# Two products of a fused attention, experts and gated-block kernel computed with seven block products in place of eight

## The chip, the cores and the metric

The kernel runs on one core of one Trainium2 chip. The metric is the device time of one execution in microseconds; times are compared as medians of several runs. One execution is also recorded by the profiler, and all rows below come from that one.

## The reference

Three stages work on 4608 tokens of 512 features. Only the third is touched by the change.

```python
attn_out = _attn_ref(q, k, v)                     # softmaxed q times (softmaxed k^T v)
x = attn_out.transpose(0, 2, 1, 3).reshape(4608, 512)
x = _moe_ref(x, modality_id, w_gate, modality_bias, w1, w2)   # one of 8 experts per token

def _moe2_ref(x, w1, w2, w3, w_out):              # 512x1024, 512x1024, 1024x1024, 1024x512
    a = x @ w1
    b = x @ w2
    h = a * b @ w3
    return (h @ w_out).astype(np.float32)
```

## The kernel before

Every float32 number that enters a large matmul is held as a high part `h` and a low part `l` (`split`, lines 833 to 835: ScalarE casts the source to the high part, then VectorE subtracts it from the source to give the low part). A product is three matmuls, high by high, low by high and high by low (`PAIRS`, line 32). A matmul takes a block of 128 by 128 as its stationary operand and streams up to 512 columns.

All steps are put into a list with estimated costs, their reads and their writes (`Plan.add`), and a list scheduler puts each engine's steps into the order in which they would start (`Plan.order`). Each engine then runs its steps in that order; waits between engines follow from the data. `P` is TensorE, `S` ScalarE, `V` VectorE, `G` GpSimd, `D` the DMAs that SyncE issues, in order, and `X` a step without an instruction.

The attention stage writes `x_dram`. The expert stage (`slot`, its matmuls on lines 645 and 665) writes its result, turned, to `yT` in DRAM (line 669). `doubles` (lines 684 to 692) turns the float64 weights of the third stage into float32 in DRAM beside it, in tiles `st`, `T`, `Q`, `O`.

The third stage first builds `w3 @ w_out`, of 1024 by 512. `stage` loads weight rows into a ring of seven tiles of 1024 columns. `turned(fb)` transposes block `fb` of `w3` on TensorE (line 849) into two PSUM banks, and `split` puts its high and low parts into one of two buffers. `product(fb)` multiplies it with `w_out` (24 matmuls on line 862), and `split` puts the result into `WP`. `first_two` loads and splits `w1` and `w2` meanwhile, a row block for each `fb`. There are eight `fb`.

Then nine units of 512 tokens follow. `positions(u)` loads one unit of `yT` and splits it. For each of eight blocks `m` of 128 features of the 1024, 12 matmuls make `a` (line 914, evicted by ScalarE on line 919) and 12 more make `b`; VectorE multiplies the two (line 921) and the product is split into `PT` (lines 834, 835). Then four blocks of 128 tokens take 24 matmuls each with `WP` (line 933), ScalarE evicts them (line 939), and GpSimd issues an indirect DMA that puts the rows at their places in the output (line 941).

## Time and profile before

| what | value |
|---|---|
| runs, median of 3 (lowest to highest) | 1299.66 us (1293.59 to 1301.91) |
| profiled execution, its own time | 1293.58 us |
| its span | 1291.9 us |
| TensorE busy | 1196.3 us, 93% |
| VectorE busy | 636.1 us, 49% |
| ScalarE busy | 450.2 us, 35% |
| GpSimd busy | 292.5 us, 23% |
| mean granted TensorE clock | 0.966 of full speed |

PE is TensorE's matmuls, PEld its loads of stationary operands, DVE VectorE, ACT ScalarE, POOL GpSimd, SP SyncE. Matmuls are pipelined: the records of two that follow each other overlap, so the rate is read from start to start or from a chain, not from the duration of one. Instructions of DVE and ACT overlap a little as well, so a run of them is shorter than the sum of its records.

### The profile page before, as it was taken

Reading aid. Unit: us, or ns where it says so; the run is one execution under the profiler, and the core shown is the slowest. Engines: PE = TensorE matmul, PEld = TensorE weight load, DVE = VectorE, ACT = ScalarE, POOL = GpSimd, SP = SyncE. Lnnn points to the kernel's source line nnn. Section 1 sums busy time; section 2 is a strip of 40 time slices with the busy share of each in tenths; the row PEclk is TensorE's granted clock in tenths of the full one; section 3 lists DMA queues with packets and bytes.
Section 4 is the critical chain, followed back from the end, with each engine's and each line's share of the span. In section 5 each row is a group of like instructions: output and inputs, shape, how many; then the busy total and the mean of one; then the engine's idle time right before and its main releaser. Section 6 shows DMA issues by size and latency. Waiting matters only on the chain.

```text
span 1291.9 us, 19827 instructions
## 1 busy us (share of the span) xinstructions
PE 1196.3 (93%) x8035; PEld 1007.5 (78%) x8035; DVE 636.1 (49%) x1100; ACT 450.2 (35%) x841; POOL 292.5 (23%) x286
## 2 busy tenths in 40 slices
...
GB/s 355 392 260 69 53 244 130 250 211 208 138 127 188 204 235 136 222 271 157 207 145 33 15 51 6 60 2 64 1 66 1 65 1 65 1 65 1 33 1 33
DMA packets 67960, 153.94 MB, mean 119 GB/s; under 512 B 11758, under 2 KB 14354, under 8 KB 67858
## 3 DMA queue, kind: packets, MB, share of 16 engines
...
HBM read 129.67 MB, written 39.70 MB: 131 GB/s over the span
## 4 chain that ended last, share of the span: by engine, by line
PE 68%; DVE 2%; issue 1%; ACT 1%; DMA 0%; POOLq 0%; ACTq 0%; DVEq 0%
PE pb L914 30%; PE pb L933 15%; PE pb L665 11%; PE pb L645 8%; PE pb L862 3%; DVE w2l L591 1%; PE pb L628 1%; PE pb L849 0%; DVE xt L688 0%; ACT w2h L589 0%; DVE xt L686 0%; DVE hTl L650 0%; DMA out_dram<-misc,oall 0%; DVE xt L687 0%; DVE xt L685 0%
## 5 line engine op out<-in xcount | busy, mean ns | idle before, releaser
L921 DVE TENSOR_TENSOR xg<-xg,pb 128x512 f32<-128x512 f32 x72 | 49.5, 688 | 405.8 <-PE pb L914 400.5
L941 POOL DMA_INDIRECT out_dram<-misc,oall x36 | 35.0, 973 | 626.4 <-ACT misc L939 626.4
L645 PE MATMUL pb<-xTh,w1h 128*128 128x512 f32 (+1 forms) x384 | 134.5, 350 | 3.9 <-DVE hTl L650 3.9
L665 PE MATMUL pb<-hTh,w2h 128*128 128x512 f32 (+1 forms) x384 | 134.6, 350 | 0.0
L665 PE MATMUL pb<-hTl,w2h 128*128 128x512 f32 (+1 forms) x384 | 133.4, 347 | 0.0
L645 PE MATMUL pb<-xTl,w1h 128*128 128x512 f32 (+1 forms) x384 | 133.3, 347 | 0.1
L665 PE MATMUL pb<-hTh,w2l 128*128 128x512 f32 (+1 forms) x384 | 133.2, 347 | 0.0
L645 PE MATMUL pb<-xTh,w1l 128*128 128x512 f32 (+1 forms) x384 | 132.9, 346 | 0.0
L834 ACT CAST pTh<-xg 128x512 fp32r<-128x512 f32 x76 | 46.9, 620 | 197.3 <-DVE xg L921 197.3
L914 PE MATMUL pb<-xTh,hTh 128*128 128x512 f32 x288 | 112.1, 389 | 0.0
L914 PE MATMUL pb<-xTl,hTh 128*128 128x512 f32 x288 | 112.0, 389 | 0.0
L914 PE MATMUL pb<-xTh,hTl 128*128 128x512 f32 x288 | 112.0, 389 | 0.0
L914 PE MATMUL pb<-xTh,w1h 128*128 128x512 f32 x288 | 112.0, 389 | 0.0
L914 PE MATMUL pb<-xTl,w1h 128*128 128x512 f32 x288 | 112.0, 389 | 0.0
L914 PE MATMUL pb<-xTh,w1l 128*128 128x512 f32 x288 | 112.0, 389 | 0.0
L933 PE MATMUL pb<-w2h,pTh 128*128 128x512 f32 x288 | 112.0, 389 | 0.0
L933 PE MATMUL pb<-w2l,pTh 128*128 128x512 f32 x288 | 112.0, 389 | 0.0
L933 PE MATMUL pb<-w2h,pTl 128*128 128x512 f32 x288 | 112.0, 389 | 0.0
L649 ACT ACTIVATE hTh<-pb 128x512 fp32r<-128x512 f32 (+1 forms) x96 | 48.9, 510 | 116.8 <-PE pb L645 116.4
L645 PEld LDWEIGHTS pb<-xTh,w1h 128*128 128x128 f32 x384 | 73.1, 190 | 14.1 <-DVE hTl L650 5.1
L645 PEld LDWEIGHTS pb<-xTl,w1h 128*128 128x128 f32 x384 | 73.1, 190 | 9.4 <-DVE xTl L633 0.6
L665 PEld LDWEIGHTS pb<-hTh,w2l 128*128 128x128 f32 x384 | 73.1, 190 | 9.1
...
## 6 DMA issues: line engine op xcount, KB each, us to landing
...
```

Of the source, the lines that this page charges most:

```text
L591: P.add(g, c, lambda: e.tensor_tensor(lo(), raw(), hi().bitcast(F32), op=ALU.subtract), r=[K(nm + "r", i), K(nm + "h", i), extra], w=[K(nm ...
L628: PE.transpose(p[:, kk, 128 * t : 128 * t + 128], xg[h][:, t, c : c + 128], ident)
L645: PE.matmul(p(), lhsT=W1(i)[:, TURN[kk], ms], rhs=XT(z)[:, kk, cols], start=(kk == 0 and c == 0), stop=(kk == 3 and c == 2))
L649: P.add("S", ps_(N), lambda hh=hh, p=p: SC.activation(hh(), p(), AF.Relu), r=[K("bk", pb), "Mb"], w=[K("hh", h, m) for h in hs])
L665: PE.matmul(p(), lhsT=W2(i)[:, f, ns], rhs=HT(y)[:, f, cols], start=(f == 0 and c == 0), stop=(f == 7 and c == 2))
L834: P.add("S", (ps_ if psum else sb_)(n), lambda: SC.copy(hi(), src), r=sk, w=[hk])
L862: PE.matmul(bank[pb], lhsT=th[i][:, 8 * p2 + g], rhs=PT(y)[:, g], start=(g == 0 and n == 0), stop=(g == 7 and n == 2))
L914: PE.matmul(dst, lhsT=mat[i][:, kk, ms], rhs=XT[z][:, kk], start=(c == 0), stop=(c == 11))
L921: P.add("V", vt_(512), lambda a_=a_, p_=p_, p2=p2: V.tensor_tensor(p_, a_, bank[p2], op=ALU.mult), r=[K("bk", p2), K("a", wb), K("ring", 1 ...
L933: PE.matmul(bank[pb], lhsT=PT(i)[:, f, ts], rhs=WP[y][:, f], start=(c == 0), stop=(c == 23))
L941: P.add("G", (1.04, 0.74), lambda o3=o3, c=c: G.indirect_dma_start(out=out, out_offset=bass.IndirectOffsetOnAxis(ap=oall[:, c : c + 1], ax ...
```

## The change

`x @ w1` and `x @ w2` are each cut into two by two blocks and computed by Strassen's algorithm in Winograd's form: seven block products in place of eight, with four sums of weight blocks, four sums of token blocks, and seven sums of products. The unit is 768 tokens, six units in all; the two halves of a unit (384 tokens each) are the column blocks, the two halves of the 512 features the inner blocks.

`factors(a, t)` takes the place of `first_two`. It is called four times, for `fb` 0 to 3, loads two ring tiles, makes four sums on GpSimd, and splits seven factors of 512 columns each (28 splits in all, where there were 16). They lie in `ar`, one tile that takes the place of the expert stage's weight and activation tiles. The ring has five tiles, now all carved from one tile `ca`, which also holds the staging tiles of the earlier stages (`xt`, `xg` and smaller ones).

`positions(b)` loads the four blocks of a unit, makes four differences on VectorE and splits seven blocks of 768 columns (2 by 384). There is one set of these split blocks.

`quarter(b, f, a)` computes 128 features of both halves of the 1024 for both token halves: seven products of six matmuls of 384 columns each into four banks, and their sums. `a` 0 is `x @ w1`, `a` 1 is `x @ w2`, and with `a` 1 the sums are multiplied into those of `a` 0. Two sets of four banks alternate. The result goes to `p_dram` in DRAM.

`w3 @ w_out` goes to `wp_dram` in DRAM, copied by ScalarE. After the sixth unit a phase of its own loads `wp_dram` and, in chunks of 512 tokens by 512 features, `p_dram`, splits both (`arrive`, `weights`, `tokens`), and does the nine times four blocks of 24 matmuls as before, with four banks in place of two and two sets of split products.

Other parts of the diff only rename or place tiles: `ones` in the pool of the even batches, `w_out`'s split parts and the turned `w3` in `al`, `thm` and `tt`.

```diff
+CA, FILL, AL = 9440, 20, 9216
+BT = 768
+HB = BT // 2
...
+    wp_dram = dr.tile([1024, 512], F32, name="wp_dram")
+    p_dram = dr.tile([1024, NTOK], F32, name="p_dram")
...
+        ar = M["ar"] = pb.tile([128, 28672], F32R, name="ar")
+        part = lambda a, k, f: ar[:, a : a + k * f].rearrange("p (k f) -> p k f", k=k)
+        M["W1"] = [part(4096 * i, 4, 1024) for i in range(2)]
+        M["XT"] = [part(8192 + 2048 * i, 4, 512) for i in range(2)]
+        M["W2"] = [part(12288 + 4096 * i, 8, 512) for i in range(2)]
+        M["HT"] = [part(20480 + 4096 * i, 8, 512) for i in range(2)]
+        M["thm"] = pb.tile([128, 2 * BT], F32R, name="thm")
         M["pb"] = pb
+        M["py"] = tc.alloc_tile_pool(name="yo", bufs=1, side="right", reuse_waits="tile")
+        M["yo"] = M["py"].tile([128, 4, 2 * TS], F32, name="yo")
...
+    ar = M["ar"]
...
+    def wide_a():
         M["pr"].release()
         M["pm"] = tc.alloc_tile_pool(name="moe2", bufs=1, reuse_waits="tile")
-        M["PT"] = [M["pm"].tile([128, 8, 512], F32R, name=f"pT{i}") for i in "hl"]
-
...
+        M["al"] = M["pm"].tile([128, AL], F32R, name="al")
+
+    def wide_b():
+        M["py"].release()
+        M["pt"] = tc.alloc_tile_pool(name="turn", bufs=1, side="right", reuse_waits="tile")
+        M["tt"] = M["pt"].tile([128, 2048], F32R, name="tt")
+
+    def wide_c():
+        M["pt"].release()
+        M["px"] = tc.alloc_tile_pool(name="sums", bufs=1, side="right", reuse_waits="tile")
+        M["sx"] = M["px"].tile([128, 4 * HB], F32, name="sx")
+
+    P.add("X", 0.0, wide_a, w=two("w1r", 8) + two("w2r", 8) + ["Mc"])
+    P.add("X", 0.0, wide_b, w=[K("yo", b, i) for b in range(2) for i in range(4)] + ["Me"])
+    hand_over(["Mc"], two("wo", 8) + two("wol", 8) + [K("th", 0), K("tl", 0)])
+    hand_over(["Me"], [K(x, i) for x in ("th", "tl") for i in (2, 3)])
+    old = [K(x, i) for x in ("w1h", "w1l", "w2h", "w2l") for i in range(8)] + [K(x, b, i) for x in ("hh", "hl") for b in range(2) for i in range(8)]
+    old += [K("xh", b, i) for b in range(2) for i in range(2)] + [K("xl", b, i, "t") for b in range(2) for i in range(2)]
+    hand_over(old, two("Mf", 4))
+    hand_over([K(x, i) for x in ("st", "T", "Q", "O") for i in range(2)] + [K("xg", b, i) for b in range(2) for i in range(2)], two("ring", 5) + two("tmp", 4) + two("ev", 2))
+    ring = [(ca[:, 1024 * i : 1024 * i + 1024], [K("ring", i)]) for i in range(5)]
+    tmp = [flat(ca[:, 5120 + 512 * i : 5632 + 512 * i], 4) for i in range(4)]
+    evict = [ca[:, 8416 + 512 * i : 8928 + 512 * i] for i in range(2)]
+    WO = lambda i, g: M["al"][:, 1024 * g + 512 * i : 1024 * g + 512 * i + 512]
+
+    def th(i, q, g=0, n=4):
+        t, a = (("al", 8192), ("thm", 0), ("tt", 0), ("tt", 1024))[q]
+        a += 512 * i + 128 * g
+        return flat(M[t][:, a : a + 128 * n], n)
...
-        t, kk = ring[rot("ring", 7)]
+        t, kk = ring[rot("ring", 5)]
...
-                for g in range(4 * z, 4 * z + 4):
+                for g in range(4):
                     for n, (i, y) in enumerate(PAIRS):
-                        PE.matmul(bank[pb], lhsT=th[i][:, 8 * p2 + g], rhs=PT(y)[:, g], start=(g == 0 and n == 0), stop=(g == 7 and n == 2))
...
+                        PE.matmul(bank[pb], lhsT=th(i, 2 * p2 + z, g, 1)[:, 0], rhs=WO(y, 4 * z + g), start=(z == 0 and g == 0 and n == 0), stop=(z == 1 and g == 3 and n == 2))
+
+            P.add("P", 2.73, mm, r=[K(x, 2 * p2 + z) for x in ("th", "tl")] + [K(x, g) for g in range(4 * z, 4 * z + 4) for x in ("wo", "wol")], w=[K("bk", pb)])
+        P.add("S", ps_(512), lambda: SC.copy(evict[p2], bank[pb]), r=[K("bk", pb)], w=[K("ev", p2)])
+        P.add("D", 0.7, lambda: SP.dma_start(wp_dram[128 * fb : 128 * fb + 128], evict[p2]), r=[K("ev", p2)], w=[K("wpd", fb)])
...
+    A11, A12, A22, S1, S2, S3, S4 = range(7)
+    B11, T1, T3, T2, B21, B22, T4 = range(7)
+    PRODUCTS = ((A11, B11, 0), (S1, T1, 2), (S3, T3, 3), (S2, T2, 1), (A12, B21, 0), (S4, B22, 2), (A22, T4, 3))
+    Mt = ar[:, 0:28672].rearrange("p (f a i s t c) -> p f a i s t c", f=4, a=2, i=2, s=7, t=2)
+
+    def factors(a, t):
+
+
+        r0, k0 = stage(f"m{a + 1}", t)
+        r1, k1 = stage(f"m{a + 1}", t + 2)
+        mk = lambda i, m: K("M", a, t, i, m)
+        at = lambda i, m: Mt[:, :, a, i, m, t]
+        q = {A11: flat(r0[:, 0:512], 4), A12: flat(r1[:, 0:512], 4), A22: flat(r1[:, 512:1024], 4)}
+        a21 = flat(r0[:, 512:1024], 4)
+        both = k0 + k1
+        sk = {A11: both, A12: both, A22: both}
+
+        def sum_(n, m, x, y, op, r):
+            P.add("G", gt_(512), lambda: G.tensor_tensor(tmp[n], x, y, op=op), r=r, w=[K("tmp", n)])
+            q[m], sk[m] = tmp[n], [K("tmp", n)]
+
+        sum_(0, S1, a21, q[A22], ALU.add, both)
+        sum_(1, S3, q[A11], a21, ALU.subtract, both)
+        sum_(2, S2, tmp[0], q[A11], ALU.subtract, both + [K("tmp", 0)])
+        sum_(3, S4, q[A12], tmp[2], ALU.subtract, both + [K("tmp", 2)])
+        for m in (A11, S1, S3, S2, A12, S4, A22):
+            P.add("S", sb_(512), lambda m=m: SC.copy(at(0, m), q[m]), r=sk[m] + two("Mf", 4), w=[mk(0, m)])
+            P.add("V", vt_(512), lambda m=m: V.tensor_tensor(at(1, m), q[m], at(0, m).bitcast(F32), op=ALU.subtract), r=sk[m] + [mk(0, m)] + two("Mf", 4), w=[mk(1, m)])
...
-        first_two(1 + fb // 4, fb % 4)
...
+        if fb < 4:
+            factors(fb // 2, fb % 2)
...
+    P.add("X", 0.0, wide_c, w=two("th", 4) + two("tl", 4) + ["Md"])
+    hand_over(["Md"], [K("s", i) for i in (2, 3, 4, 5)] + [K("Xh", 6), K("Xl", 6)])
+    hand_over([K(x, g) for x in ("wo", "wol") for g in range(3)], [K(x, i) for x in ("Xh", "Xl") for i in (0, 1)])
+    hand_over([K(x, g) for x in ("wo", "wol") for g in range(3, 8)], [K(x, i) for x in ("Xh", "Xl") for i in range(2, 6)])
+    hand_over(two("tmp", 4), two("raw", 4))
+    hand_over(two("ring", 5), [K("raw", i) for i in (4, 5, 6)] + two("pa", 3) + [K("s", 1)])
+    hand_over(two("ev", 2), [K("pa", 3), K("s", 0)])
...
+    S_ = lambda i: sums[i] if i < 2 else M["sx"][:, HB * (i - 2) : HB * (i - 1)]
+
+    def X(i, x):
+        t, n = (M["thm"], i) if x == T4 else (M["al"], 2 * x + i)
+        return flat(t[:, BT * n : BT * n + BT], 2)
+
+    RAW = {B11: 0, B21: 1, B22: 2, T3: 3, T1: 4, T2: 5, T4: 6}
+    B12 = 3
+
+    def positions(b):
+        src = yT[:, BT * b : BT * b + BT].rearrange("(j n p) t -> p j n t", p=128, j=2)
+        for n, (j, k) in ((RAW[B11], (0, 0)), (B12, (0, 1)), (RAW[B22], (1, 1)), (RAW[B21], (1, 0))):
+            P.add("D", 1.2, lambda n=n, j=j, k=k: SP.dma_start(raw[n], src[:, j, :, HB * k : HB * k + HB]), r=["yT"], w=[K("raw", n)])
...
+        def diff(to, x, y):
+            P.add("V", vt_(768), lambda: V.tensor_tensor(raw[to], raw[x], raw[y], op=ALU.subtract), r=[K("raw", x), K("raw", y)], w=[K("raw", to)])
+
+        diff(RAW[T1], B12, RAW[B11])
+        diff(RAW[T3], RAW[B22], B12)
+        diff(RAW[T2], RAW[B22], RAW[T1])
+        diff(RAW[T4], RAW[B21], RAW[T2])
+        for _, x, _ in PRODUCTS:
+            n = RAW[x]
+            split(raw[n], [K("raw", n)], lambda x=x: X(0, x), lambda x=x: X(1, x), K("Xh", x), K("Xl", x), 768)
...
+    def quarter(b, f, a):
+
+
+        z = (2 * f + a) % 2
+        bk = lambda j: bank[4 * z + j][:, 0:HB]
+        bkk = lambda j: K("bk", 4 * z + j)
+        S = lambda j: S_(3 * z + j)
+        sk = lambda j: K("s", 3 * z + j)
+        seen = set()
+        for m, x, j in PRODUCTS:
+
+            def mm(m=m, x=x, j=j, fresh=j not in seen):
+                for t in range(2):
+                    for n, (i, y) in enumerate(PAIRS):
+                        PE.matmul(bk(j), lhsT=Mt[:, f, a, i, m, t], rhs=X(y, x)[:, t], start=(fresh and t == 0 and n == 0), stop=(t == 1 and n == 2), skip_group_check=not fresh)
+
+            seen.add(j)
+            P.add("P", 1.04, mm, r=[K("Mf", f), K("Xh", x), K("Xl", x)] + [K("M", a, t, i, m) for t in range(2) for i in range(2)], w=[bkk(j)])
+            for c, (mine, to) in enumerate(((A11, 0), (S1, 1), (S3, 2))):
+                if m == mine:
+                    P.add("S", ps_(HB), lambda j=j, to=to: SC.copy(S(to), bk(j)), r=[bkk(j)], w=[sk(to)])
+            if m == S2:
+                P.add("V", vt_(HB), lambda: V.tensor_tensor(S(0), S(0), bk(1), op=ALU.add), r=[bkk(1)], w=[sk(0)])
+                P.add("G", gt_(HB), lambda: G.tensor_tensor(S(1), S(1), S(2), op=ALU.add), r=[sk(2)], w=[sk(1)])
+        p0, p1 = f % 2, 2 + f % 2
+        lo, hi = slice(0, HB), slice(HB, BT)
+        o0, o1 = pa[p0], pa[p1]
+        if a == 0:
+            P.add("S", ps_(HB), lambda: SC.copy(o0[:, lo], bk(0)), r=[bkk(0)], w=[K("pa", p0)])
+            P.add("V", vt_(HB), lambda: V.tensor_tensor(o0[:, hi], S(0), bk(2), op=ALU.add), r=[sk(0), bkk(2)], w=[K("pa", p0)])
+            P.add("V", vt_(HB), lambda: V.tensor_tensor(o1[:, lo], S(0), bk(3), op=ALU.add), r=[sk(0), bkk(3)], w=[K("pa", p1)])
+            P.add("G", gt_(HB), lambda: G.tensor_tensor(o1[:, hi], S(0), S(1), op=ALU.add), r=[sk(0), sk(1)], w=[K("pa", p1)])
+        else:
+            P.add("G", gt_(HB), lambda: G.tensor_tensor(S(1), S(0), S(1), op=ALU.add), r=[sk(0)], w=[sk(1)])
+            P.add("G", gt_(HB), lambda: G.tensor_tensor(o1[:, hi], o1[:, hi], S(1), op=ALU.mult), r=[sk(1)], w=[K("pa", p1)])
+            P.add("V", vt_(HB), lambda: V.tensor_tensor(o0[:, lo], o0[:, lo], bk(0), op=ALU.mult), r=[bkk(0)], w=[K("pa", p0)])
+            P.add("V", vt_(HB), lambda: V.tensor_tensor(S(2), S(0), bk(2), op=ALU.add), r=[sk(0), bkk(2)], w=[sk(2)])
+            P.add("V", vt_(HB), lambda: V.tensor_tensor(o0[:, hi], o0[:, hi], S(2), op=ALU.mult), r=[sk(2)], w=[K("pa", p0)])
+            P.add("V", vt_(HB), lambda: V.tensor_tensor(S(2), S(0), bk(3), op=ALU.add), r=[sk(0), bkk(3)], w=[sk(2)])
+            P.add("V", vt_(HB), lambda: V.tensor_tensor(o1[:, lo], o1[:, lo], S(2), op=ALU.mult), r=[sk(2)], w=[K("pa", p1)])
+            for p_, r in ((p0, f), (p1, f + 4)):
+                P.add("D", 1.2, lambda p_=p_, r=r: SP.dma_start(p_dram[128 * r : 128 * r + 128, BT * b : BT * b + BT], pa[p_]), r=[K("pa", p_)], w=[K("pd", r, b)])
+
+    for b in range(NTOK // BT):
+        positions(b)
+        for f in range(4):
+            for a in range(2):
+                quarter(b, f, a)
...
+    hand_over(kept(0, 1), two("wph", 8))
+    hand_over(kept(1, 2), [K("ph", 0, i) for i in range(8)] + two("wpl", 8))
+    hand_over(kept(2, 3), [K("pl", 0, i) for i in range(8)] + [K("ph", 1, i) for i in range(8)])
+    hand_over(kept(3, 4), [K("pl", 1, i) for i in range(8)])
+    hand_over(two("raw", 7), two("chunk", 2) + two("o3", 2))
+    hand_over(two("pa", 4) + two("s", 2), [K("chunk", 2), K("o3", 2), K("o3", 3)])
...
+    def arrive(src, r, to, hk, lk, first):
+        n = rot("chunk", 2 if first else 3)
+        P.add("D", 2.9, lambda: SP.dma_start(chunks[n], src.rearrange("(n p) t -> p n t", p=128)), r=r, w=[K("chunk", n)])
+        for f in range(4):
+            split(chunks[n][:, f], [K("chunk", n)], lambda f=f: to(0, f), lambda f=f: to(1, f), hk(f), lk(f), 512)
+
+    def weights(h):
+        arrive(wp_dram[512 * h : 512 * h + 512], [K("wpd", 4 * h + f) for f in range(4)], lambda i, f: WP(i, 4 * h + f), lambda f: K("wph", 4 * h + f), lambda f: K("wpl", 4 * h + f), True)
+
+    def tokens(u, h):
+        z = u % 2
+        bs_ = sorted({512 * u // BT, (512 * u + 511) // BT})
+        arrive(p_dram[512 * h : 512 * h + 512, 512 * u : 512 * u + 512], [K("pd", 4 * h + f, b) for f in range(4) for b in bs_], lambda i, f: PB(z, i, 4 * h + f), lambda f: K("ph", z, 4 * h + f), lambda f: K("pl", z, 4 * h + f), u == 0)
+
+    for h in range(2):
+        weights(h)
+        tokens(0, h)
...
-            def mm(dst, mat, ms=ms):
-                c = 0
-                for kk in range(4):
-                    for i, z in PAIRS:
-                        PE.matmul(dst, lhsT=mat[i][:, kk, ms], rhs=XT[z][:, kk], start=(c == 0), stop=(c == 11))
-                        c += 1
-
-            P.add("P", 2.6, lambda mm=mm, p1=p1: mm(bank[p1], M1), r=yk + [K(x, 1, kk, m // 4) for x in ("mh", "ml") for kk in range(4)], w=[K("bk", p1)])
-            first = [K("ring", 1 + wb)] if u == 0 and m < 2 else []
-            P.add("S", ps_(512), lambda a_=a_, p1=p1: SC.copy(a_, bank[p1]), r=[K("bk", p1)], w=[K("a", wb)] + first)
-            P.add("P", 2.6, lambda mm=mm, p2=p2: mm(bank[p2], M2), r=yk + [K(x, 2, kk, m // 4) for x in ("mh", "ml") for kk in range(4)], w=[K("bk", p2)])
-            P.add("V", vt_(512), lambda a_=a_, p_=p_, p2=p2: V.tensor_tensor(p_, a_, bank[p2], op=ALU.mult), r=[K("bk", p2), K("a", wb), K("ring", 1 + wb)], w=[K("p", wb)])
-            split(p_, [K("p", wb)], *both(lambda i, m=m: PT(i)[:, m]), K("ph", m), K("pl", m), 512)
...
+            for h in range(2):
+                tokens(u + 1, h)
...
+            for f in range(8):
+
+                def mm(f=f, ts=ts, z=z, u=u):
+                    for n, (i, y) in enumerate(PAIRS):
+                        PE.matmul(bank[z], lhsT=PB(u % 2, i, f)[:, ts], rhs=WP(y, f), start=(f == 0 and n == 0), stop=(f == 7 and n == 2))
+
+                P.add("P", 0.68, mm, r=[K("ph", u % 2, f), K("pl", u % 2, f), K("wph", f), K("wpl", f)], w=[K("bk", z)])
+            P.add("S", ps_(512), lambda z=z: SC.copy(o3[z], bank[z]), r=[K("bk", z)], w=[K("o3", z)])
```

## Rows read from the trace of the kernel before

**Rows 1.** The page's head: the whole span, busy time by engine.

```profile
span 1291.9 us, 19827 instructions
...
PE 1196.3 (93%) x8035; PEld 1007.5 (78%) x8035; DVE 636.1 (49%) x1100; ACT 450.2 (35%) x841; POOL 292.5 (23%) x286
```

**Rows 2.** Windows by stage: stretch, busy us by engine, clock, DMA.

```profile
core 0: us, PE busy (x) PEld busy (x) DVE busy (x) ACT busy (x) POOL busy (x), PEclk, DMA share, GB/s
...
638.30:692.33 54.03, 51.19 (x258) 42.49 (x256) 27.50 (x45) 23.74 (x45) 0.00 (x0) 1.00 0.35 119
692.33:1280.05 587.72, 587.72 (x2592) 486.33 (x2592) 118.37 (x178) 125.82 (x211) 34.04 (x35) 1.00 0.09 31
1280.05:1291.90 11.85, 0.00 (x0) 0.00 (x0) 0.00 (x0) 0.59 (x1) 0.97 (x1) 0.61 0.06 22
```

**Rows 3.** Chain that ended last, in time order: start, us, work.

```profile
626.72 11.54 PE pb L665 x96
...
641.20 2.78 PE pb L862 x12
...
672.55 0.87 PE pb L849 x8
...
679.77 10.92 PE pb L862 x48
...
690.72 0.59 ACT w2h L834
...
1193.01 21.76 PE pb L933 x96
1214.77 43.52 PE pb L914 x192
```

**Rows 4.** Timeline of PE, 256 columns: first and last of sixty.

```profile
614.26 0.28 PE L645 MATMUL pb<-xTh,w1h 128*128 128x256 f32 x1
...
621.34 0.28 PE L645 MATMUL pb<-xTh,w1l 128*128 128x256 f32 x1
```

**Rows 5.** Timeline of DVE: 256-column steps, then a 512-column pair.

```profile
622.00 0.41 DVE L690 TENSOR_SCALAR xt<-xt 128x512 int32<-128x512 int32 x1
622.34 0.41 DVE L650 SCALAR_TENSOR_TENSOR hTl<-pb,hTh 128x256 fp32r<-128x256 f32 x1
622.67 0.68 DVE L691 SCALAR_TENSOR_TENSOR xt<-xt 128x512 f32<-128x512 int32 x1
...
639.81 1.28 DVE L835 TENSOR_TENSOR xTl<-pb,xTh 128x512 fp32r<-128x512 f32 x2
```

**Rows 6.** Timeline of ACT: one cast of 512, then two.

```profile
638.54 0.62 ACT L834 CAST hTh<-xt 128x512 fp32r<-128x512 f32 x1
...
642.06 1.16 ACT L834 CAST hTh<-xt 128x512 fp32r<-128x512 f32 x2
```

**Rows 7.** Timeline of DVE beside POOL's sums.

```profile
614.65 1.79 DVE L686 SCALAR_TENSOR_TENSOR xt<-xt,xt 128x512 int32<-128x512 int32 x1
616.37 0.68 DVE L591 TENSOR_TENSOR w2l<-w2r,w2h 128x512 fp32r<-128x512 f32 x1
...
617.64 1.58 DVE L688 SCALAR_TENSOR_TENSOR xt<-xt,xt 128x512 f32<-128x512 uint32 x1
```

**Rows 8.** Timeline of POOL in the same stretch.

```profile
614.11 1.79 POOL L591 TENSOR_TENSOR w2l<-w2r,w2h 128x512 fp32r<-128x512 f32 x1 [4.80 <-ACT w2h L589]
617.39 1.29 POOL L591 TENSOR_TENSOR w2l<-w2r,w2h 128x512 fp32r<-128x512 f32 x1 [1.49 <-ACT w2h L589]
```

**Rows 9.** Line 591 on DVE and POOL: min, median, max ns.

```profile
L591 DVE TENSOR_TENSOR w2l<-w2r,w2h x72: 673/691/2190, 182.6 to 621.1; 128x512 fp32r<-128x512 f32 x72
...
L591 POOL TENSOR_TENSOR w2l<-w2r,w2h x24: 1275/1356/1867, 198.4 to 617.4; 128x512 fp32r<-128x512 f32 x24
```

**Rows 10.** Timeline of SP's DMA issues at the stage's start.

```profile
623.38 0.34 SPq L692 DMA_DIRECT2D m_f<-xt  x1
...
638.67 0.40 SPq L669 DMA_DIRECT2D yT<-yo  x1
```

120 lines of the change are left out of this document (42 added, 78 removed).

## The prediction

> **What bounds the kernel now.** Read the page's head first: TensorE is busy 93% of the span, VectorE 49% [rows 1]. Such shares are averages over stages, so the next view is the windows by stage. In the stretch that the change rewrites, 692.33 to 1280.05, PE is busy 587.72 of 587.72 us at a granted clock of 1.00; DVE is busy 118, ACT 126, POOL 34, and the DMA share is 0.09 [rows 2]. The chain of waits says the same: from 692.33 on it is PE alone, 43.52 us for 192 matmuls of line 914, then 21.76 for 96 of line 933, nine times [rows 3]. So each matmul removed there is time removed, so long as PE stays fed. The stage ahead, 638.30 to 692.33, has PE busy 51.19 of 54.03 with DVE at 27.5 [rows 2]; it is near PE's bound too, and the change puts more work on DVE and POOL there. The last view is the timelines: the step of a matmul by its columns, and what DVE does while POOL works.
>
> **The price of a matmul of 384 columns.** The trace has none. With 512 columns a step is 43.52/192 = 226.7 ns [rows 3]. With 256 columns, sixty matmuls start between 614.26 and 621.34: 7.08/59 = 120.0 ns [rows 4]. A line through both has 0.417 ns a column (the 2.4 GHz level) and 13.3 ns fixed, so 384 columns take 173.3 ns. If cost were proportional to columns it would be 170.0 by the first row and 180.0 by the second; these are my ends. I take 173.3, since both rows lie on that line and 384 is midway between them. The 256-column rows also come in groups of three with waits of their own, and still step at 120.0, so I put the waits of a group of six at nothing; if they cost a tenth of a microsecond, 336 groups would be 34 us.
>
> **The two products.** Removed: 9 x 192 = 1728 matmuls, 391.7 us. Added: 6 units x 8 quarters x 7 products x 6 = 2016, at 173.3 ns 349.4 us (342.7 to 362.9). The change is -42.2 us (-49.0 to -28.8). The 864 matmuls of the last phase stay, 9 x 21.76 = 195.8.
>
> **Who feeds them.** A DVE step takes 0.33 us at 256 columns and 0.60 at 512 (a pair takes 1.28, one 0.68) [rows 5], so about 0.47 at 384 and 0.87 at 768. An ACT cast steps at 1.16 - 0.62 = 0.54 for 512 [rows 6], about 0.8 for 768. A POOL sum of 512 takes 1.29 [rows 8]; 384 lies between half of it and all, and I take 1.0. Per quarter PE needs 42 x 0.1733 = 7.28 us. DVE has 3 or 6 sums, 4.5 x 0.47 = 2.1, and an eighth of a unit's eleven steps (four differences, seven splits), 11 x 0.87 / 8 = 1.2: 3.3 us. POOL has 2 or 3 sums, 2.5 us. ACT has 3 or 4 copies and its casts, some 2.5. All fit behind PE, and two sets of four banks give each eviction a whole quarter.
>
> The seven split blocks of a unit exist once. Block x of the next unit may be written only when product x of the last quarter is done, and is needed when product x of the next quarter starts, 6.24 us later. The chain for one block is 0.8 on ACT and 0.87 on DVE. Together DVE must put through seven splits and some six sums, 7 x 0.87 + 6 x 0.47 = 8.9 us, in the 11.7 us from 5.44 before the unit's end (the first cast done) to 6.24 after it (the seventh block needed). That fits, with 2.8 us to spare. But POOL's sums beside it stretch DVE: with POOL's sum running from 617.39 to 618.68, a DVE step that otherwise takes 0.68 took 1.58, and 1.79 beside the one from 614.11 [rows 7, 8]; line 591 has a median of 691 ns and a longest of 2190 [rows 9]. So each POOL sum costs DVE about a microsecond when it has two operands in SBUF. Three sums fall into that time: 3 against 2.8. I take 0.5 us at each of the five changes of unit, 2.5 in all (0 to 15, the 15 if all three microseconds land on PE).
>
> The Trainium skill, SBUF — State Buffer, section "SBUF: two separate sides", speaks against putting sums on GpSimd here: it calls the port pair of VectorE and GpSimd an exclusive lock, by which the one that starts first holds it for its whole instruction and a VectorE operation with two SBUF inputs blocks. The trace agrees: the stretched step ended 0.54 us after POOL's. By the rule a step would lose up to the whole sum, 1.29 us rather than my 1.0, and the changes of unit would cost about a microsecond more each.
>
> **The stage of w3 @ w_out.** Each `fb` has 0.87 us of transposes and 5.46 of matmuls on PE, 6.33 [rows 3]. DVE's splits go from 16 + 8 + 16 = 40 to 16 + 28 = 44, which alone is nothing. But the 28 fall on `fb` 0 to 3, with four POOL sums each: 9 x 0.60 + 4 x 1.0 = 9.4 us per `fb` against 6.33, so DVE falls 3.1 us behind per `fb`, 12.3 in four. The splits of the turned `w3` stand in the same queue, and PE waits for these; they are ready about 4 us before PE needs them, so PE pays between 0 and 8. Ring loads queue on SP behind these splits, five tiles in place of seven. The loads of `w_out` now wait for the last `doubles` store, issued at 623.38 [rows 10], some 15 us ahead of the stage, and this I cost at nothing, 2 us if that cover is gone. Buffers 2 and 3 of the turned `w3` wait for the store of `yo` issued at 638.67 [rows 10], which lands before `product(1)` needs them. A gain is possible too, as PE idles 2.8 us of this stage now. I take +3 (-2 to +10), nearer the low end, since `fb` 4 to 7 hold two splits each and pay the backlog back.
>
> At its end PE now waits from 690.72 for the last split of `WP` and a small transpose, until 692.33 [rows 2, 3]: 1.6 us. That split goes to DRAM and away from the path; late instead are the first unit's blocks, as most of their room holds `w_out` until `product(7)` ends. Block x comes 0.87 us after the last one, under the 1.04 of a product. I take 0.5 us of the 1.6, so -1.1 (-1.6 to +1.5).
>
> **The last phase.** Splits of `wp_dram` and the first tokens need room that `quarter` frees feature block by feature block; the last 14.6 us before the phase hold eight of these splits at 0.6 and one load of 1 MB, so I take 0.5 us (0 to 3). Afterwards each 21.76 us of PE covers eight splits, 4.8 us of DVE. New DRAM traffic, two times 19 MB over 545 us, is 70 GB/s on top of 31, where the DMA share is 0.09 at those 31 [rows 2]; hidden. The tail after PE's end, 11.8 us, stays. The earlier stages only get other addresses: 0.
>
> **Sum.** -42.2 + 2.5 + 3 - 1.1 + 0.5 = -37.3 us. The profiled execution took 1293.58 (span 1291.9), so it would become 1256.3. It is the fastest of the three runs shown; from their median, 1299.66, it is 1262.4. As a median after may lie at either, I say 1259.
>
> **The rivals.**
> (1) DVE and POOL hold PE up, in part: twice the stalls, a backlog of 8 in the `w3` stage and 3 at each change of unit, give -42.2 + 8 + 15 + 2 = -17, so 1276 to 1283. For it: the rows of stretched steps. Against: DVE and POOL together need 5.8 of 7.28 us per quarter even if they never overlapped.
> (2) The same lock decides each quarter, and the kernel gets slower. From 7.28 us on, every microsecond more per quarter costs 48; it takes 7.28 + 37.3/48 = 8.06 us of DVE and POOL per quarter to lose everything. With every sum at POOL's longest, 1.87, a quarter needs 3.3 + 2.5 x 1.87 = 8.0, and with one DVE step of the longest kind, 2.19 in place of 0.47 [rows 9], 9.7: 48 x 2.4 = 115 us come back, 78 slower than before, some 1375. Against: in the median a step is at 691 ns and a sum at 1.36, which leaves 1.5 us per quarter.
> (3) The matmul's cost is mostly fixed, so more and shorter ones save nothing. At 226.7 x 1728/2016 = 194.3 ns for 384 columns the gain is zero and the time 1298 to 1305, with the other terms. Against: the 256-column rows, at 120.0. The Trainium skill, TensorE: Matmul & The Clock Gate, section "Back-to-back issue gap", has such a rule: a sustained 81 ns at 128 columns and 131 at 512, whose line gives about 114 at 384, and with it 2016 short ones cost as much as 1728 long ones within 4 us. The trace does not agree: 226.7 at 512.
> (4) It doesn't do what it says: were a product computed twice or the eighth kept, 48 x 1.04 = 50 us would come back, +13: 1306 to 1312. The loops of the diff show seven.
>
> **How the numbers follow.** Forecast 0.74 (1247 to 1272: the sum with stalls between nothing and twice mine, from either base); rival 1 0.13; rival 2 0.05; rival 3 0.03; rival 4 0.01; better than the forecast, by cost proportional to columns, 0.04. The range must take in part of rival 1 and the ends of the unknown costs: 1246 to 1281. A measurement of this kernel tells about 1% from no change. Faster by over 1% is the forecast, the better case and most of rival 1: 0.88; within 1% the rest of it and part of rivals 2 and 3: 0.06; slower 0.06.
>
> **What would show it.** Right: matmuls of 384 columns stepping at 173 ns, quarters of 7.28 us without gaps, a last phase still at 21.76 us per unit. The `w3` stage should take 52 to 60 us from 638.3 on, with DVE solid in its first half. Wrong: PE idle at each change of unit for more than a microsecond, released by a split's low part; quarters longer than 7.3 us, released by evictions on DVE; a step of 180 ns or more; the granted clock below 1.00 after such gaps; PE waiting for chunks in the last phase.

## The result: 33 us faster, the forecast's gain less two terms

The changed kernel takes 1265.08 us in the median of four runs (1263.78 to 1266.9), the kernel before 1298.41 in four runs taken beside them: ratio 0.9747, 95% interval 0.9712 to 0.9782. The forecast was 1259 us in a range of 1246 to 1281. The two profiled executions differ by less than the medians (33.3 us), by 30.3 us of span, since that of the kernel before was 4.8 us below its median and that of the changed one 1.3 us below its own. Line numbers below are the changed kernel's: the quarters' matmuls are line 1002, the last phase 1078, `product` 895, the transpositions of `w3` 882, `split` 870 and 871, the splits in `factors` 928 and 929, its sums 920.

The page's head and the windows by stage (columns as in [rows 2]):

```profile
span 1261.6 us, 21370 instructions
...
PE 1161.3 (92%) x8323; PEld 1038.9 (82%) x8323; DVE 765.8 (61%) x1286; ACT 507.5 (40%) x963; POOL 453.6 (36%) x422
```

```profile
639.58:697.83 58.25, 53.92 (x258) 43.73 (x256) 40.77 (x46) 28.83 (x53) 25.64 (x16) 0.97 0.56 182
697.83:701.47 3.64, 2.58 (x15) 1.88 (x13) 2.36 (x4) 3.32 (x6) 0.00 (x0) 1.00 0.26 82
701.47:1053.89 352.42, 352.42 (x2005) 352.42 (x2006) 189.97 (x289) 117.15 (x221) 136.34 (x120) 1.00 0.26 89
```

PE is still busy all through the rewritten stretch at clock 1.00, with DVE at 190 of 352 us and POOL at 136. The stage of `w3 @ w_out` has grown from 52.5 [rows 3: 638.26 to 690.72] to 58.25 us, and POOL is busy in 25.6 of them. The chain of waits shows where:

```profile
661.74 4.02 DVE ar L929 x4
...
670.91 0.61 DVE al L871
...
671.57 4.14 PE pb L895 x10
...
686.72 11.12 PE pb L895 x48
697.83 1.06 PE pb L1002 x6
698.89 0.19 PE pb L949
...
699.11 0.03 DVE oall L950
...
699.22 0.96 DVE ca L978
...
701.47 352.42 PE pb L1002 x2004
1053.89 190.46 PE pb L1078 x840
```

Where the chain before ran over PE alone from 679.77 on [rows 3], it now goes over DVE's line 929 up to 671.57, then loses time between 697.83 and 701.47, and from there on is PE alone again to the end. The new step of a matmul stands in the timeline of PE, and that the quarters run without stalls in the groups of instructions (busy us, mean ns, idle before and its releasers):

```profile
721.60 6.50 PE L1002 MATMUL pb<-al,ar 128*128 128x384 f32 x36
727.94 1.20 PE L1002 MATMUL pb<-thm,ar 128*128 128x384 f32 x6
728.98 1.22 PE L1002 MATMUL pb<-al,ar 128*128 128x384 f32 x6
```

```profile
L1002 PE MATMUL pb<-al,ar 128*128 128x384 f32 x1728 | 312.6, 338 | 1.1 <-ACT sx L1008 0.8 <-DVE oall L950 0.3
...
L1002 PE MATMUL pb<-thm,ar 128*128 128x384 f32 x288 | 57.7, 335 | 0.0
```

36 matmuls that stream from `al` take 727.94 - 721.60 = 6.34 us, 176.1 ns each; the six that stream from `thm` take 1.04, 173.3 ns each. In all 2016 matmuls PE was idle 1.1 us, at the first quarter. A quarter is 7.38 us, not 7.28.

From these rows the 30.3 us are made up as follows: products -37.4 (2016 in 354.3 us, where 1728 took 391.7), the stage of `w3 @ w_out` +5.8, the start of the quarters +0.2 (356.06 us from 697.83 to 1053.89, of which 354.25 are 48 quarters, so 1.8 lost, where 1.6 were lost before), the last phase 0 (190.46 for 840 matmuls, 226.7 ns each as before), the late start of the stage +1.3 (639.58 against 638.26). Sum -30.1. (In some of the groups of runs below every kernel, the one before too, ran some 20 us shorter. In their profiles the difference lies ahead of the first expert matmul, which starts at 164.7 to 171.0 us there and at 186.3 to 189.2 in the others; why is open. One run of the kernel before took 3034 us and is left out of the ratios.)

Three theories for the missing 7 us were tried. **Place**: the step of 176.1 ns comes from where in SBUF the two operands start. **Backlog**: POOL's sums and the crowding of `factors` into `fb` 0 to 3 make the low parts of the turned `w3` late. **Queue**: the first unit's differences stand in DVE's queue behind a cast that waits for PE. Against each stood a rival, named with the runs.

### The profile page after: what moved, and what is told of

It is laid out like the page before. It is cut to its first block, busy times and chain, and to the rows that moved or that the text cites. A ratio compares the mean times of both kernels' runs of the same rounds, so it can differ in the third digit from the quotient of the medians.

```text
span 1261.6 us, 21370 instructions
## 1 busy us (share of the span) xinstructions
PE 1161.3 (92%) x8323; PEld 1038.9 (82%) x8323; DVE 765.8 (61%) x1286; ACT 507.5 (40%) x963; POOL 453.6 (36%) x422
## 4 chain that ended last, share of the span: by engine, by line
PE 65%; DVE 4%; issue 1%; ACT 1%; DMA 0%; POOLq 0%; ACTq 0%; DVEq 0%
PE pb L1002 28%; PE pb L1078 15%; PE pb L682 11%; PE pb L662 8%; PE pb L895 2%; DVE ar L929 2%; DVE ar L608 1%; PE pb L645 1%; DVE ca L705 0%; ACT ar L606 0%; DVE ca L703 0%; PE pb L882 0%; DVE ar L667 0%; DMA out_dram<-ca,oall 0%; DVE ca L704 0%
## 5 line engine op out<-in xcount | busy, mean ns | idle before, releaser
L1002 PE MATMUL pb<-al,ar 128*128 128x384 f32 x1728 | 312.6, 338 | 1.1 <-ACT sx L1008 0.8
L1002 PEld LDWEIGHTS pb<-al,ar 128*128 128x128 f32 x1728 | 304.5, 188 | 1.6 <-ACT sx L1008 1.1
L662 PE MATMUL pb<-ar 128*128 128x512 f32 (+1 forms) x1152 | 216.0, 347 | 4.0 <-DVE ar L667 3.9
L682 PE MATMUL pb<-ar 128*128 128x512 f32 (+1 forms) x1152 | 217.2, 347 | 0.0
L662 PEld LDWEIGHTS pb<-ar 128*128 128x128 f32 x1152 | 184.9, 190 | 32.0 <-DVE ar L667 5.1
L682 PEld LDWEIGHTS pb<-ar 128*128 128x128 f32 x1152 | 183.7, 190 | 25.7
L1078 PE MATMUL pb<-ar 128*128 128x512 f32 x864 | 196.0, 389 | 0.0
L1078 PEld LDWEIGHTS pb<-ar 128*128 128x128 f32 x864 | 162.2, 188 | 33.6
L871 DVE TENSOR_TENSOR ar<-ca,ar 128x512 fp32r<-128x512 f32 x80 | 54.9, 706 | 111.3 <-ACT ar L870 111.3
L706 POOL TENSOR_TENSOR ca<-ca 128x512 f32<-128x512 f32 x40 | 56.0, 1404 | 79.3 <-DVE ca L705 73.8
L667 DVE SCALAR_TENSOR_TENSOR ar<-pb,ar 128x512 fp32r<-128x512 f32 (+1 forms) x96 | 54.6, 570 | 40.2 <-ACT ar L666 40.1
L608 DVE TENSOR_TENSOR ar<-w2r,ar 128x512 fp32r<-128x512 f32 x72 | 59.8, 860 | 28.3 <-ACT ar L606 27.6
L608 DVE TENSOR_TENSOR ar<-w1r,ar 128x512 fp32r<-128x512 f32 x72 | 59.5, 859 | 7.5 <-DMA ord<-order_dram 3.8
```

The lines of the kernel that those rows point to most:

```text
L608: P.add(g, c, lambda: e.tensor_tensor(lo(), raw(), hi().bitcast(F32), op=ALU.subtract), r=[K(nm + "r", i), K(nm + "h", i), extra], w=[K(nm ...
L662: PE.matmul(p(), lhsT=W1(i)[:, TURN[kk], ms], rhs=XT(z)[:, kk, cols], start=(kk == 0 and c == 0), stop=(kk == 3 and c == 2))
L667: P.add("V", vt_(N), lambda hh=hh, hl=hl, p=p: V.scalar_tensor_tensor(out=hl(), in0=p(), scalar=0.0, in1=hh().bitcast(F32), op0=ALU.max, o ...
L682: PE.matmul(p(), lhsT=W2(i)[:, f, ns], rhs=HT(y)[:, f, cols], start=(f == 0 and c == 0), stop=(f == 7 and c == 2))
L706: P.add("G", gt_(512), lambda: G.tensor_tensor(Tf, Tf, Qf, op=ALU.add), r=[K("Q", b)], w=[K("T", b)])
L871: P.add("V", vt_(n), lambda: V.tensor_tensor(lo(), src, hi().bitcast(F32), op=ALU.subtract), r=list(sk) + [hk], w=[lk])
```

## The experiments

Every ratio is against runs of the kernel before that were taken beside it; the medians of different rows are not compared, for the reason just given. The stage columns are from each chain: from the first transposition of `w3` to the end of the last `product`; all quarters' matmuls; and what the stretch between the stage's end and the last phase takes beyond that (in the kernel before, between the stage's end and the first unit). The intervals of the single repairs overlap that of the change itself, so what one edit does is read from the stages of its profiled execution.

| kernel | median us | ratio (95%) | `w3` stage | quarters | lost beside them |
|---|---|---|---|---|---|
| before | 1298.41 | 1 | 52.5 | 391.7 | 1.6 |
| the change | 1265.08 | 0.9747 (0.9712 to 0.9782) | 58.3 | 354.3 | 1.8 |
| `al` at 128 | 1258.19 | 0.9713 (0.9679 to 0.9747) | 56.5 | 349.5 | 1.8 |
| all at 0 | 1260.48 | 0.9734 (0.9705 to 0.9763) | 57.9 | 349.5 | 1.8 |
| sums on DVE | 1261.30 | 0.9736 (0.9702 to 0.9769) | 55.6 | 354.3 | 1.8 |
| turned first | 1265.37 | 0.9767 (0.9731 to 0.9803) | 56.8 | 354.3 | 1.8 |
| order rows early | 1243.96 | 0.9747 (0.9719 to 0.9775) | 59.3 | 354.3 | 0.0 |
| eight products | 1289.76 | 1.0100 (1.0073 to 1.0128) | 52.7 | 404.7 | 0.2 |
| three repairs | 1238.56 | 0.9690 (0.9664 to 0.9715) | 55.2 | 349.5 | 0.0 |
| units of 512 | 1257.72 | 0.9838 (0.9813 to 0.9863) | 58.1 | 364.8 | 1.9 |
| `factors` spread | 1244.49 | 0.9731 (0.9694 to 0.9769) | 54.9 | 354.3 | 1.8 |
| spread and repairs | 1236.16 | 0.9672 (0.9647 to 0.9696) | 52.5 | 349.5 | 4.4 |
| two more POOL sums | 1244.06 | 0.9730 (0.9697 to 0.9763) | 55.2 | 349.5 | 6.8 |
| last call earlier | 1252.39 | 0.9669 (0.9641 to 0.9697) | 52.9 | 349.5 | 0.0 |

### Place: `al` moved by 128 bytes, and everything put at 0

In the changed kernel `al` (streamed) starts at a multiple of 256 bytes in each partition, `ar` (stationary) and `thm` 128 bytes past one. A narrower `ca` moves `al` alone; a wider pad beside it moves the rest too.

```diff
-CA, FILL, AL = 9440, 20, 9216
+CA, FILL, AL = 9408, 20, 9216        # al at 128 past 256; evict moved into the gap
```

> The tile al (the streamed blocks) starts 128 bytes lower, so that it has the same place in a 256-byte grid as ar and thm (the evicted w3 @ w_out tiles move too; nothing else changes). Theory, place: the 36 matmuls of a quarter that stream from al step at 176.1 ns because of where al lies, the 6 from thm at 173.3; then all step at 173.3, a quarter takes 7.28 in place of 7.38 us, the 24 matmuls of a product(fb) 5.45 in place of 5.56, and the time falls by 48 x 0.1 + 0.8 = 5.5 us. Rival, structure: it is the seven products' waits and changes of bank, which thm's product escapes as the last one; then quarters stay at 7.38 us and the time stays within 1 us.

Its chain, the last `product` rows and the quarters:

```profile
684.62 10.92 PE pb L895 x48
...
699.17 347.68 PE pb L1002 x2004
```

347.68/2004 is 173.5 ns where the change took 352.42/2004 = 175.9, and 24 matmuls of 512 columns take 5.46 where they took 5.56. The `w3` stage is 1.8 us shorter; 0.8 of that is place, and the rest is in PE's waits, 3.3 us in place of 4.3 (the clock falls there too, behind a wait of 1.89 us).

```diff
+CA, FILL, AL = 9376, 20, 9216        # and pad 24 -> 56: al, ar, thm all at 0
```

> All tiles of the right side (ar, thm, tt) move by 128 bytes down and al by 256, so that al, ar and thm all start at a multiple of 256 bytes; before, al did and the others lay 128 off. If it is the relation of streamed and stationary operand that counts, quarters fall to 7.28 us as with al moved alone, and the last phase stays at 21.76 us per 96 matmuls. If a streamed operand that starts at a multiple of 256 bytes is slow by itself, quarters stay at 7.38 or grow to 7.40, and the last phase grows to about 22.1 us per 96, some 3 us slower in all. If place counts for nothing, all stays.

```profile
699.11 347.67 PE pb L1002 x2004
```

The same pace with every tile at 0. So it is not one place that is slow but the relation: streamed and stationary operand 128 bytes apart in the 256-byte grid cost 2.8 ns per matmul of 384 columns. Place theory holds, the price is 4.8 us in the quarters. The stage of this kernel, 57.9 us, has a wait of 2.12 us with a fall of the clock behind it, as in the change.

### Backlog: sums on VectorE, and the turned rows first

```diff
-P.add("G", gt_(512), lambda: G.tensor_tensor(tmp[n], x, y, op=op), ...)
+P.add("V", vt_(512), lambda: V.tensor_tensor(tmp[n], x, y, op=op), ...)
```

> The sixteen sums of weight blocks in factors are made on VectorE in place of GpSimd. Theory, lock: the splits of VectorE are slow in this stage because GpSimd's sums hold them up (9.4 us per fb); without them VectorE needs 13 x 0.60 = 7.8 us per fb, the stage of w3 @ w_out falls from 58.3 to 54 to 56 us, and the time by 2 to 4 us. Rival, count: VectorE has too many steps in the first four fb, whoever makes the sums; with four more per fb the stage grows by up to 4 x 2.4 = 9 us. Rival, ring: loads wait for ring tiles; the stage stays at 58.

The timeline of DVE there, a run of sums and a run of low parts:

```profile
643.38 1.88 DVE L920 TENSOR_TENSOR ca<-ca 128x512 f32<-128x512 f32 x3
...
656.94 3.69 DVE L929 TENSOR_TENSOR ar<-ca,ar 128x512 fp32r<-128x512 f32 x6
```

Beside no POOL sum the six low parts take 3.69 us, 0.60 each; in the change seven took 9.17. Although DVE now makes sixteen more instructions, it is busy 37.8 us of the stage in place of 40.8: the sums cost DVE more on POOL than on DVE itself. The stage is 2.7 us shorter, within the forecast of 54 to 56; the clock stays at 1.00 there, which alone was worth 1.8 us (see the stage's part below). The ring rival has a part in what is left: PE waits 0.60 us for a load of `w3` into a ring tile, and 0.96 for the low part that follows from it.

The other edit leaves the sums on POOL; the planner is told the true cost of the factors' low parts and puts the turned rows' casts and low parts ahead.

```diff
-P.add("V", vt_(n), lambda: V.tensor_tensor(lo(), src, ...), ...)
+P.add("V", vt_(n), lambda: V.tensor_tensor(lo(), src, ...), ..., pri=-1000 if psum else 0)   # ScalarE's cast too
...
-P.add("V", vt_(512), lambda m=m: V.tensor_tensor(at(1, m), ...), ...)
+P.add("V", vt_(512) + 0.55, lambda m=m: V.tensor_tensor(at(1, m), ...), ...)
```

> The scheduler is told that a low part of a factor costs 0.55 us more than it assumed (what GpSimd's sums add), and that the splits of the turned w3 go ahead of others that are ready. Work and tiles are the same. Theory, queue: TensorE waits since the splits of the turned w3 stand behind factors in VectorE's queue; with another order its gaps in this stage (4.3 us) and the stretch at a clock of 0.64 after the last gap (some 1.9 us) go, and the stage falls from 58.3 to 53 to 55 us; the factors end later, about 680, still ahead of the first quarter. Rival, load: whatever the order, VectorE and GpSimd together are too slow, and the wait moves to the first unit's blocks: stage shorter, start of the quarters no earlier, time within 1 us.

The stage takes 56.8 us, 1.4 less, and the clock stays at 1.00; the forecast of 53 to 55 was missed, and the time is not different from the change's. PE's longest wait in the stage is now one for a load of `w3` into a ring tile, and behind it PE stands 0.96 us for that row's low part:

```profile
677.58 1.09 PE L882 MATMUL pb<-ident,ca 128*128 128x128 f32 x8 [1.05 <-DMA ca<-w_f]
```

A kernel with more ring tiles was not run. The chain shows the relation of places once more, inside one kernel: twelve matmuls of 512 columns with both operands in `al`, then twelve with the stationary one in `thm`.

```profile
643.96 2.74 PE pb L895 x12
...
647.13 2.80 PE pb L895 x12
```

### Queue: the order rows made earlier

```diff
         if fb < 4:
             factors(fb // 2, fb % 2)
+        if fb == 5:
+            ...                          # the order rows, from oraw to oall
```

> The order rows (one small DMA, a cast on VectorE, one transposition on TensorE, the cast oall) move from behind the last product of the w3 stage to behind product(5); nothing else changes. In the changed kernel VectorE stood 4.29 us before oall, behind a transposition that TensorE did only after the first quarter's first product, and the first unit's differences stood behind oall; from the first of these 6 matmuls (697.67 us) to the unbroken run of the quarters (701.47) it took 3.80 us for 14 matmuls that need 2.4. Queue theory: with oall out of the way the differences are made while product(7) runs and that stretch shrinks to 2.4 to 2.8 us, so the time falls by 1 to 1.5 us against the changed kernel (ratio to the kernel before about 0.9737). Rival, pace of the casts: the first unit's blocks come one every 0.9 us from the casts on ScalarE whatever the queue's order, and room for them is handed over only as product(7) ends; then the stretch stays at 3.6 us or more and the time is the same.

The chain where the quarters start:

```profile
648.72 1.25 PE pb L882 x8
...
675.88 354.27 PE pb L1003 x2016
```

The quarters' 2016 matmuls follow the stage without a gap: queue theory holds, 1.8 us. The profiled execution's stage took 1.0 us more: PE waited 2.17 us for DVE's low part until 648.72, and its clock then fell as in the change. The ratio is the change's own, 0.9747; it cannot tell a gain of 1.8 us and a loss of 1.0, since its interval is 0.28% wide to either side, 3.6 us.

### Seven for eight alone

```diff
-PRODUCTS = ((A11, B11, 0), (S1, T1, 2), (S3, T3, 3), (S2, T2, 1), (A12, B21, 0), (S4, B22, 2), (A22, T4, 3))
+PRODUCTS = ((A11, B11, 0), (A21, B11, 2), (A11, B12, 1), (A21, B12, 3), (A12, B21, 0), (A22, B21, 2), (A12, B22, 1), (A22, B22, 3))
```

> The kernel is that of the change in all its parts (units of 768 positions, 48 quarters, a*b through DRAM, its own last phase), but each quarter makes the ordinary eight block products: no sums of factors, no differences of positions, no sums of products; the output is the same. Count theory (the gain is that of 7 products for 8, and the rest of the reorganization costs some us): 48 matmuls of 176.1 ns a quarter, 8.45 us, 405.7 us for the 48 against 354; the w3 stage without the sums on GpSimd takes 53 to 55 us instead of 58.2; in sum 1265 + 51.5 - 4 = 1310 to 1314, which is slower than the kernel before (ratio 1.008 to 1.013). Rival (part of the gain comes from the reorganization itself: a*b no longer split on the way, an evener load on the vector engines): below 1300.

```profile
620.87:673.60 52.73, 51.77 (x259) 42.81 (x258) 22.15 (x35) 22.77 (x42) 0.00 (x0) 1.00 0.59 208
```

```profile
674.95 403.63 PE pb L984 x2298
```

The reorganization with eight products is 1.0% slower than the kernel before. Without sums POOL does nothing, DVE has the low parts of 16 weight blocks in place of 28, and the `w3` stage is back at 52.7 us: its growth came with the sums and the twelve blocks that they add. The 13.0 us more in the quarters (2304 shorter matmuls at 175.6 ns are 404.7, against 391.7) account for the difference from the kernel before, of which some 5 us are the place of `al` once more: that a*b goes through DRAM and the last phase stands by itself shows no cost beside them. Seven products in place of eight are worth 50.4 us of PE.

### Together, and how close DVE and POOL are to the bound

The first kernel here has the three edits above, that of `al`, of the sums and of the order rows:

> The change with three repairs: al moved by 128 bytes so that streamed and stationary operand start on the same place of the 256 byte grid (alone it gave 4.7 us in the quarters and 0.8 us in the w3 stage), the sums of factors on VectorE instead of GpSimd (alone: 2.7 us in the w3 stage), and the order rows moved ahead of product(6). If the three losses are separate, they add: quarters 347.7 us instead of 352.4, w3 stage 54 to 55.5 instead of 58.2, start of the quarters 1 to 1.5 us less, in sum 1254 to 1256 (ratio 0.966 to 0.968). Rival (they overlap: a stall taken away lets another one of the same stretch show): 1257 to 1260.

The losses add by the stages: 55.2, 349.5 and nothing lost at the start, 9.6 us less than the change in all. The ratio, 0.9690, is 0.0057 under the change's, which is 7.4 us; that is outside the forecast of 0.966 to 0.968 and in the range given for the rival, while its interval, 0.9664 to 0.9715, takes in part of both.

```diff
-BT = 768
+BT = 512          # and al at 128; the planner's costs follow
```

> The change with al moved by 128 bytes and units of 512 positions instead of 768: blocks of 256 columns, 72 quarters of 42 matmuls. Price theory (a matmul costs 13.3 ns beside 0.4167 ns a column, 120.0 ns at 256 columns as in the kernel before): 3024 x 120.0 = 362.9 us against 2016 x 173.3 = 349.4, so 13.5 us more than the same kernel with units of 768, that is 1270 to 1274 (ratio 0.981 to 0.984). Lock rival: VectorE and GpSimd took 3.96 and 2.84 us of each quarter of 7.38 us; scaled to 256 columns by the parts of the rows that do not depend on columns that is about 2.65 and 2.3 us, in sum 4.95 of the 5.04 us that TensorE now needs, and with waits between them they hold TensorE up: gaps inside the quarters, 375 us or more for the stage, 1284 or more.

The window of the quarters with 256 columns (after PE, PEld come DVE, ACT and POOL):

```profile
690.47:1052.23 361.76, 361.76 (x3000) 360.56 (x3001) 206.72 (x426) 129.52 (x321) 141.18 (x180) 1.00 0.26 87
```

2999 matmuls in 361.76 us, 120.6 ns each, against the 120.0 of [rows 4]; the price theory holds at a second size, and the ratio lies where it put it. PE is never idle, although DVE and POOL together are busy 206.7 + 141.2 = 348 of 362 us.

```diff
     P.add("G", gt_(HB), lambda: G.tensor_tensor(S(1), S(1), S(2), op=ALU.add), ...)
+    for _ in range(2):                   # with the three repairs
+        P.add("G", gt_(HB), lambda: G.tensor_tensor(S(2), S(2), S(2), op=ALU.add), ...)
```

> The three repairs, and in each quarter two more sums of 384 columns on GpSimd (a block of sums that is no longer needed, added to itself; the output is the same). There a quarter of 7.28 us held 3.93 us of VectorE and 2.84 of GpSimd; one sum takes GpSimd 1.02 us when nothing is beside it, so it becomes 3.93 + 4.9 = 8.8 us. Lock rival of the prediction (work of the two engines excludes each other, and the quarter is as long as their sum): 48 quarters of 8.8 us, 420 us, and the kernel is slower than before by about 1%. Theory from the rows (a VectorE instruction with an operand in PSUM kept its 0.55 us beside a GpSimd sum; only those with both operands in SBUF were stretched, and these are under 2 us a quarter): GpSimd's 4.9 us and those 2 us fit, the quarters stay at 349.5 to 351 us, ratio 0.969 as without the two sums.

Windows of all quarters, and the timelines at a change of unit, of DVE, POOL and PE in order of time:

```profile
680.06:1036.31 356.25, 350.89 (x2018) 349.29 (x2017) 206.04 (x285) 118.53 (x224) 227.06 (x215) 1.00 0.25 88
```

```profile
736.76 4.52 DVE L871 TENSOR_TENSOR al<-ca,al 128x768 fp32r<-128x768 f32 x3
...
740.42 1.73 POOL L1025 TENSOR_TENSOR ca<-ca,sx 128x384 f32<-128x384 f32 x1
...
741.20 0.54 DVE L1027 TENSOR_TENSOR sx<-sx,pb 128x384 f32<-128x384 f32 x1
...
744.18 1.58 DVE L871 TENSOR_TENSOR thm<-ca,thm 128x768 fp32r<-128x768 f32 x1
...
745.81 0.62 PE L1003 MATMUL pb<-thm,ar 128*128 128x384 f32 x2 [1.07 <-DVE thm L871]
```

DVE and POOL are busy 206 + 227 = 433 us in 356: their busy times overlap, and the quarters did not become as long as the sum (48 x 9.0 us). The instruction with an operand in PSUM (741.20) keeps its 0.54 us while POOL's sum of 740.42 runs, and none of the 168 of this kind in the quarters takes more than 0.56; splits with all operands in SBUF are stretched, three took 4.52 us (in the change three in a row take 2.69) and the last 1.58 (0.95 there), and PE waits 1.07 us for that one at the change of unit. That makes 6.8 us in all, more than the rows' theory gave (0 to 1.5) and a tenth of what the lock rival gave (70). (The added sums write a block that DVE's line 1027 needs as well; DVE waits for them 25.8 us in 16 of the 48 quarters, and PE has no gap there.) The Trainium skill, SBUF — State Buffer, section "SBUF: two separate sides", names for the lock VectorE operations with two SBUF inputs and those in a 2-port mode; these rows agree on the first kind and say nothing on the second.

### The same work in other places of the stage

```diff
-        if fb < 4:
-            factors(fb // 2, fb % 2)
+        if fb % 2 == 0:
+            factors(fb // 4, fb // 2 % 2)
```

> The change with one edit: the four calls of factors (sums on GpSimd, casts on ScalarE, low parts on VectorE) stand behind the products 0, 2, 4 and 6 of the w3 stage instead of 0, 1, 2 and 3. The work, its engines and its count are the same. Backlog theory (a call with its beside-GpSimd price takes VectorE about 9 us, two rows of w3 take TensorE 12.6 us: four calls in a row push VectorE behind, so that the low parts of the transposed rows come late; every second row leaves it room): the gaps of TensorE in the stage shrink from 4.3 us to 2 or less, the clock does not fall, the stage takes 54 to 55.5 us instead of 58.2 to 59.3, ratio to the kernel before 0.971 to 0.973. Lock rival (the price is GpSimd's sums themselves, wherever they stand): the stage stays at 57 us or more. Third: the last call now ends so late that the first unit's blocks or the second quarter wait: what the stage gains is lost at the start of the quarters.

```profile
622.82:677.67 54.85, 52.10 (x257) 42.66 (x256) 39.25 (x46) 28.49 (x53) 24.02 (x16) 1.00 0.58 193
```

With POOL's sums as in the change, 24.0 us of them, PE now idles 2.75 us in place of 4.33, the granted clock is 1.00 throughout and the stage takes 54.9: spacing alone takes away 3.4 of the 5.8 us. The rival, that the sums cost the same wherever they stand, falls. The ratio, 0.9731, is at the edge of what was forecast.

This edit and the three repairs together:

> The three repairs together (al moved by 128 bytes, sums of factors on VectorE, order rows early) and the four calls of factors behind products 0, 2, 4 and 6. Backlog theory: the stage takes 52.5 to 53.5 us, as with eight products and no sums (52.7), against 55.2 with the three repairs alone, the quarters 349.5 as there: ratio 0.966 to 0.9675, the best version. Rival: what is won in the stage is lost as the quarters start, since raw blocks and the first unit's differences now stand behind the last call: ratio 0.969 as with the three repairs.

Gaps of PE at the start of the quarters, and the cast on ACT behind them:

```profile
675.26 0.44 PE L1003 MATMUL pb<-al,ar 128*128 128x384 f32 x1 [1.45 <-ACT al L870]
676.25 3.27 PE L1003 MATMUL pb<-al,ar 128*128 128x384 f32 x12 [0.55 <-DVE al L871]
```

```profile
676.85 3.77 ACT L870 CAST al<-ca 128x768 fp32r<-128x768 f32 x5 [1.64 <-DMA ca<-yT]
```

The stage is 52.5 us, and 4.4 us are lost behind it: the first blocks of positions land late, since their buffers hold the last call's sums; 2.3 us are waits, the rest a granted clock of 0.73 and 0.70 behind them (676 to 679 and 679 to 682 us). The stage was as the theory says and the start as the rival says, and by the stages their sum is the rival's, 406.4 us against 404.7 with the three repairs. The ratio, 0.9672, lies in the theory's range but cannot be told from the three repairs' 0.9690. The last kernel has the three repairs and another spacing:

```diff
-        if fb < 4:
-            factors(fb // 2, fb % 2)
+        if fb in (0, 2, 3, 5):
+            c = (0, 2, 3, 5).index(fb)
+            factors(c // 2, c % 2)
```

> The three repairs with the four calls of factors behind products 0, 2, 3 and 5. With 0, 1, 2 and 3 the w3 stage took 55.2 us and the quarters began without a gap; with 0, 2, 4 and 6 the stage took 52.7 us, but the first quarter then stood 3.7 us in all, since its blocks arrive through buffers that the last call's sums hold until about 668 us, 5.8 us before the stage's end. Theory (both waits are of places, not of work): one product earlier frees these buffers 6 us sooner, the blocks are there in time, and the backlog of one pair of calls in a row (2 us) is covered by the product ahead: stage 52.7 to 53.7 us, first quarter's loss 0.5 us or less, about 2 us less than with the three repairs, ratio 0.967 to 0.968. Rival: the pair 2 and 3 already makes the low parts of a transposed row late (stage 54.5 us or more), and the time stays that of the three repairs, 0.969.

```profile
687.25 0.20 PE pb L949
...
687.47 0.21 DVE oall L950
...
687.81 5.72 PE pb L895 x24
693.53 349.46 PE pb L1004 x2016
```

Stage 52.9 us, no gap behind it, ratio 0.9669: the best version by its stages (12.0 us under the change in the last three columns of the table), and its interval lies below the change's. Against the three repairs and against the spread with them it is not separated by the times. Its stage still has 0.6 us in which PE transposes the order rows and waits for the cast.

## Why the prediction was right, and where its sum was off

The forecast came true by its own mechanism: PE alone sets the stretch, fewer columns streamed is time gained, and the gain is the seven for eight (with eight products the kernel is slower than before). Of the sum of -37.3, -30.1 came by the profiled executions and -33.3 by the medians. The sum is closer than its terms: four of them came out 10.2 us worse together (the products 4.8, the stage 2.8, the start 1.3, the earlier stages 1.3) and two 3.0 us better, so part of its closeness is luck: errors of both signs.

**Price of 384 columns.** The line through [rows 3, 4] held: 173.3 ns from `thm`, 173.5 once `al` was moved, 120.6 with 256 columns. Mis-sized was the term of the two products, -37.4 in place of -42.2, because 1728 of the 2016 stream from a tile that lies 128 bytes off their stationary operand in the 256-byte grid; with `al` moved the term is the forecast's -42.2 (349.5 against 391.7). No row of the trace before could show it, since in all its large matmuls the two tiles share their place. The ends of 170.0 and 180.0 covered it. Rival 3 stays contradicted by the measured 173.3. The Trainium skill, TensorE: Matmul & The Clock Gate, section "Back-to-back issue gap", has a sustained 81 ns at 128 columns and 131 at 512; an estimate from these two is about 114 at 384, and these runs do not agree with it.

**Changes of unit.** Forecast +2.5, measured 0. The prediction had the condition, "each POOL sum costs DVE about a microsecond when it has two operands in SBUF". The step that failed is the next one, "Three sums fall into that time: 3 against 2.8", which charges every sum in full, whatever DVE does beside it. At each of the five changes of unit two of the seven splits were stretched, from 0.95 to some 1.47 and 1.32 us, 0.9 us together and within the 2.8 to spare; the sums that read PSUM were not. The first change:

```profile
757.07 1.47 DVE L871 TENSOR_TENSOR al<-ca,al 128x768 fp32r<-128x768 f32 x1
758.46 0.54 DVE L1024 TENSOR_TENSOR sx<-sx,pb 128x384 f32<-128x384 f32 x1
758.92 1.32 DVE L871 TENSOR_TENSOR al<-ca,al 128x768 fp32r<-128x768 f32 x1
...
760.63 0.95 DVE L871 TENSOR_TENSOR al<-ca,al 128x768 fp32r<-128x768 f32 x1
```

The run with two more POOL sums has the stalls that the forecast had described, for the reason that it named.

**The stage of `w3 @ w_out`.** Forecast +3 (-2 to +10), measured +5.8. The mechanism was right, DVE behind by the sums and by crowding. The timeline of DVE in the change, that of PE at its two long waits, and PE's only wait in the stage of the kernel before:

```profile
641.88 7.00 DVE L929 TENSOR_TENSOR ar<-ca,ar 128x512 fp32r<-128x512 f32 x5
648.80 1.27 DVE L871 TENSOR_TENSOR tt<-pb,tt 128x512 fp32r<-128x512 f32 x2
...
661.74 9.17 DVE L929 TENSOR_TENSOR ar<-ca,ar 128x512 fp32r<-128x512 f32 x7
670.83 0.68 DVE L871 TENSOR_TENSOR al<-pb,al 128x512 fp32r<-128x512 f32 x1
```

```profile
649.58 1.21 PE L882 MATMUL pb<-ident,ca 128*128 128x128 f32 x8 [1.49 <-issue]
...
671.57 4.14 PE L895 MATMUL pb<-al 128*128 128x512 f32 x10 [1.88 <-DVE al L871]
```

```profile
640.55 0.66 PE L849 MATMUL pb<-ident,xt 128*128 128x128 f32 x4 [1.44 <-DVE xTl L835]
```

The low parts of the first three calls of `factors`, 21, with those of six turned blocks between them, take DVE from 641.88 to 670.83, 29.0 us, against 3 x 9.4 = 28.2 reckoned. PE stood 0.96, 1.49 and 1.88 us; for the 1.49 the profile names no releaser, but the transpositions there write the bank that the first low part of 648.80 reads, and start as it ends. That is 4.3 us in place of 1.4, the +3 of the forecast. What it had left out came on top: 1.8 us because the granted clock fell behind the longest wait, and 0.8 us for the place of `al`; 0.3 us of the 5.8 are not accounted for. The window behind the longest wait:

```profile
672.00:674.50 2.50, 2.50 (x7) 1.98 (x6) 2.50 (x5) 0.62 (x1) 0.33 (x1) 0.50 0.56 207
```

PE had waited 1.88 us; then it ran at 0.50, the 1.2 GHz level, and ten matmuls took 4.14 us where 48 take 11.12, so ten 2.32; from 676.00 on the clock is at 1.00 again.

**Start of the quarters.** Forecast -1.1, measured +0.2. The step "Block x comes 0.87 us after the last one" overlooked what stands ahead of the blocks in DVE's queue: `oall`, which waits for a transposition that PE makes behind the first product. Moved, the loss is zero.

**The last phase** cost 0 in place of 0.5, and the earlier stages differed by +1.3 us between the two executions, which lies within what the executions of these kernels show there (the first expert matmul starts at 186.3 to 189.2).

**Rivals 1 and 2** asked whether DVE and POOL hold PE up. In the stage ahead they do. In the quarters they do not, though 256 columns or two more sums bring them to 348 of 362 and 433 of 356 us. The point given for rival 2, 8.06 us of both engines per quarter, is wrong as a rule: at 9.0 us per quarter the quarters lost 6.8 us, not 48 times the difference, for only a part of DVE's instructions was stretched by POOL.
